# Left-over rows of a top-1 expert layer: grouped by expert over pairs of batches

## The chip, the cores and the metric

The kernel runs on one core of a Trainium2 chip. The metric is the time of one execution on the device in microseconds; what is compared is the median of several runs. The profile is one execution taken by the hardware profiler. Engines: PE multiplies matrices and writes PSUM banks, ACT, DVE and POOL work on vectors, SP issues most DMAs, POOL issues the indirect ones.

## The reference

Agent attention, then an expert layer in which each row goes to one expert:

```python
B, N, C = 4, 11456, 128        # 49 agents per batch; 8 experts, hidden size 1024
a2k = softmax(agents @ k.T / sqrt(C));  agent_v = a2k @ v       # 49 averages per batch
q2a = softmax(q @ agents.T / sqrt(C));  x = q2a @ agent_v       # one row per query
logits = x @ w_gate;  e = argmax(logits)
gate = softmax(logits)[e];  eom = 1 / (1 + exp(-(x @ w_output_gate)))
out = gate * eom[e] * (relu(x @ w1[e]) @ w2[e])                 # per row, by its expert e
```

## The kernel before

**Main stream.** For each batch the kernel picks one expert, the one that most rows choose, and computes all rows of the batch with it. A batch has 12 units of 1024 rows (the last has 192), a unit two tiles of 512. In a tile, `mm1` makes hidden values `h` from the softmax weights of the queries (`x_ld`) and the averages already multiplied into w1 (`w`); ACT writes `hh`, DVE the remainder `hl`; `mm2` multiplies both by w2 (`vv`) into `y`; ACT, DVE and POOL scale `y` into `os`, and SP stores it. Rows that belong to another expert ("left rows") get a wrong result here, and are written over later.

**Around it.** While a batch's main products run, the keys and values (`ks`, `av`) of the next batch and the queries (`qs`, then `q_rest`) of units ahead are worked on. A query unit may start once the main stream is at most four units behind it (`roomy`, `AHEAD = 5`). `q_rest` ends in a table of which rows chose which expert; `q_tail`, after a batch's last unit, counts them (`cum`, `tot`) and stores the running counts (`cumd`). The softmax weights of all rows go to DRAM (`efd`), and so do the 49 averages of a batch (`avnd`).

**Left rows.** They are gathered into tiles of 128 rows, one expert to a tile. `PHASES` holds (first batch, batches, static tiles, rows of the table): phase 0 is batches 0 to 2 with 13 tiles, phase 1 batch 3 with one. In a tile all rows are of one batch and one expert, so a phase has up to 8 groups for each of its batches. For a phase:

- `left_prepare` waits for the counts, calls `left_table` (which tile holds which group, and from which row of it on), and then `left_index` for 3, 4, 4 and 2 tiles at a time. These use the space of batch 3's key scores (`S0` to `S3`), so each call also waits until that part of the scores has been used. Phase 1 has one call.
- `left_index` finds for each of the 128 rows of a tile where it stands: the group's running counts by partition (product `pbs`), the partition and the rest by comparisons on DVE, a gather of a row of `cumd`, more comparisons, and a gather of the row's weights from `efd` into `ef`.
- `left_load` loads the averages of the tile's batch (`lav`) and the expert's w1 and w2 (`lw_ld`), for which it needs two of the 7 large load places that the loads of q, k and v use too. Those loads go first.
- `left_front` turns `ef` (product `let`) and multiplies it by the averages (`lx`, result `lxs`). `left_back` makes the hidden values (8 products `lh`) and the output (8 products `ly`), all in fp32. `left_store` scatters 128 rows to the output.

Two ways (`left_static`) each take every second tile, one after another. The last phase's `left_back` waits until the main stream has ended. Behind it stands a loop for tiles beyond the static ones.

**Order.** It is fixed when the program is built, by a planner. Each piece of work is a generator that asks for one instruction at a time; a clock of expected times (`Clock`) and priorities decide who goes next. Main products are emitted in turn, and `tick` puts at most one other fp32 product behind each. Relu work and the like has priority 0, `left_prepare` 1, `q_rest` 2, the fronts of left tiles 4, their backs 5. After an indirect DMA, score products (`block`) pause for 4.5 us.

Of the kernel before, what the change touches and what calls it, by code (L numbers as in the profile page):

```python
# [17 lines left out]
P = 128  # L18
# [11 lines left out]
PHASES = [(0, 3, 13, 384), (3, 1, 1, 128)]  # L30
# [15 lines left out]
K_OWN = 309  # L46
K_DUP = 310
K_W = 311
# [220 lines left out]
def agent_attention_top1_moe(ctx, tc, qT, kT, v, aT, wg, wo, w1, w2, cst, out):  # L269
# [94 lines left out]
    ticol = kc[:, K_TI:K_TI + 4]  # L364
# [1014 lines left out]
    def left_table(ph):  # L1379

        b0, nb, _, rows = PHASES[ph]
        ng, kr = nb * E, rows // P
        tt_ = tot[:, b0 * E:b0 * E + ng]

        def row(n, w=NG, dt=F32):
            return lt(n, [w], f"_{ph}", [min(w, ng)], dt)

        def cube(n):
            return lt(n, [4, NG], f"_{ph}", [kr, ng])
# [5 lines left out]
        ppi = row("ppi")  # L1395
# [6 lines left out]
        cnt = row("cntsb")  # L1402
# [10 lines left out]
        t0, ni, ti_ = row("t0"), row("t2"), row("t1i", NG, I32)  # L1413
# [3 lines left out]
        yield from DVE.q.tensor_tensor_scan(ni, ones[:, 0:ng], t0, 0.0, op0=ALU.mult, op1=ALU.add)  # L1417
        yield from DVE.q.tensor_scalar(ni, ni, 1.0 / 128.0, None, op0=ALU.mult)
        tt = lt(f"tt{ph}", [4, 8], f"_{ph}", [kr, 8])
        yield from POOL.q.memset(tt, 0.0)  # L1420
        ti = ticol[:, 0:kr]
        bc3 = [P, kr, ng]
# [5 lines left out]
        ne = lt("ne", [4], f"_{ph}", [kr])  # L1428
# [3 lines left out]
        yield from DVE.q.tensor_tensor(cm, iota32[:, 0:ng].unsqueeze(1).broadcast_to(bc3), g_.unsqueeze(2).broadcast_to(bc3), op=ALU.is_equal)  # L1432
        yield from DVE.q.tensor_tensor(cm2, cm, cnt.unsqueeze(1).broadcast_to(bc3), op=ALU.mult)
        yield from DVE.q.tensor_reduce(tt[:, :, 2], cm2, axis=AX.X, op=ALU.add)
        yield from DVE.q.tensor_scalar(g_, g_, float(ng - 1), None, op0=ALU.min)
# [7 lines left out]
        tti = lt("tti", [4, 8], f"_{ph}", [kr, 8], I32)  # L1443
# [3 lines left out]
        yield from DVE.q.tensor_copy(nti[ph], ni[:, ng - 1:ng])  # L1447

        yield from DVE.q.tensor_scalar(over[:, ph:ph + 1], ni[:, ng - 1:ng], float(PHASES[ph][2]), None, op0=ALU.is_gt)
# [3 lines left out]
    def left_index(ph, i, n, nm, got=None, big=None):  # L1453
# [11 lines left out]
        if own:  # L1465
# [12 lines left out]
            eq = lt("leq", [NSTM], nm, [n])  # L1478
# [6 lines left out]
            yield from PE.q.matmul(t[:, 0:n * P], ones[0:ng, :], c[0:ng].rearrange("p n k -> p (n k)"), start=True,  # L1485
                                   stop=True)
            yield from ACT.q.copy(pb.rearrange("p n k -> p (n k)"), t[:, 0:n * P])
            release(mark)
        else:
# [5 lines left out]
            gr = nc.values_load(ti[0:1, 0, 0:1], engines=[SP], min_val=0, max_val=ng - 1,  # L1495
                                skip_runtime_bounds_check_because=WHY)
            yield from SY.q.dma_start(pb[:, 0, :], ppid[ph][bass.ds(gr, 1), :].broadcast_to([P, P]))

        def col(m):
            return lt("l" + m, [NSTM], nm, [n])  # L1500
# [3 lines left out]
        yield from DVE.q.tensor_tensor(inv, r, tb[:, :, 2], op=ALU.is_ge)  # L1504
        rb = r.unsqueeze(2).broadcast_to([P, n, P])
# [4 lines left out]
        ppx = col("ppx")  # L1510
# [5 lines left out]
        yield from DVE.q.scalar_tensor_tensor(rg, tb[:, :, 0], 128.0, row, op0=ALU.mult, op1=ALU.add)  # L1516
        ru = lt("lru", [NSTM], nm, [n], U32)
# [20 lines left out]
        yield from DVE.q.scalar_tensor_tensor(t, tb[:, :, 4], float(N), t, op0=ALU.mult, op1=ALU.add)  # L1538
# [8 lines left out]
        o0 = n * NCOL  # L1547
# [5 lines left out]
        for k in range(n):  # L1553
# [3 lines left out]
            if got:  # L1557
                got(k, clk.ready[big.name] + (2000.0 if n > 1 else 0.0), ti, tg, ef, oa)
            yield from pause(1500.0 if n > 1 else 0.0)
        return ti, tg, ef, oa  # L1560

    def left_load(ph, ti, k, nm, at_=None):
        b0, nb, _, _ = PHASES[ph]
        yield from SY.wait(ti)
        er = nc.values_load(ti[0:1, k, 3:4], engines=[SP], min_val=0, max_val=E - 1,
                            skip_runtime_bounds_check_because=WHY)
        yield from SY.wait(ti)
        br = nc.values_load(ti[0:1, k, 4:5], engines=[SP], min_val=0, max_val=nb - 1,
                            skip_runtime_bounds_check_because=WHY)
        av = wk.tile([P, C], F32, name=f"lav{nm}", tag="l_av")  # L1570
        yield from SY.q.dma_start(av[0:A], avnd[b0:b0 + nb][bass.ds(br, 1)].rearrange("a p c -> p (a c)"))
# [10 lines left out]
        return av, w1t, w2t  # L1582
# [7 lines left out]
    def left_front(nm, ef, av):  # L1590
# [10 lines left out]
        yield from PE.q.matmul(x[:, 0:P], av[0:A], et[0:A], start=True, stop=True)  # L1601
# [37 lines left out]
    ready = {}  # L1639

    def left_prepare(ph):

        b0, nb, nst, _ = PHASES[ph]
        while counted[0] < b0 + nb:
            yield None
        yield from left_table(ph)
        i = 0
        for j, n in enumerate((3, 4, 4, 2) if nst > 2 else (nst,)):
# [7 lines left out]
            def got(k, t, ti, tu, ef, oa, i=i):  # L1656
                ready[ph, i + k] = t, ti, k, tu[:, k:k + 1], ef[:, k, :], oa[:, k, :]
# [11 lines left out]
    def left_static(way):  # L1669
# [8 lines left out]
        def fronts():  # L1678
            for i, (ph, k) in enumerate(todo):
                while (ph, k) not in ready or i > finished[0]:  # L1680
                    yield None
                t, ti, kk, _, ef, _ = ready[ph, k]
                yield from pause(t - clk.now())
                av, w1t, w2t = yield from left_load(ph, ti, kk, f"{ph}_{k}", left_place)
                yield from pause(max(clk.ready[x.name] for x in (av, w1t, w2t)) - clk.now())
                xs = yield from left_front(f"{ph}_{k}", ef, av)
# [3 lines left out]
        for ph, k in todo:  # L1690
# [5 lines left out]
            _, _, _, tu, ef, oa = ready[ph, k]  # L1696
# [48 lines left out]
    with tc.For_i(0, some, 1):  # L1745
        for ph, (b0, nb, nst, rows) in enumerate(PHASES):
            nr = nc.values_load(nti[ph][0:1, 0:1], min_val=0, max_val=rows,
                                skip_runtime_bounds_check_because="at most one tile per 128 tokens and one per group")
            with tc.For_i(nst, nr, 1) as i:
                ti, tu, ef, oa = drain(left_index(ph, i, 1, f"d{ph}"))  # L1750
                av, w1t, w2t = drain(left_load(ph, ti, 0, f"d{ph}"))
                xs = drain(left_front(f"d{ph}", ef[:, 0, :], av))
# [14 lines left out]
def _consts():  # L1767
# [42 lines left out]
```

## Time and profile before

| | |
|---|---|
| median of 3 runs | 976.49 us (975.86 to 976.65) |
| profiled execution, time | 976.57 us |
| profiled execution, span from first to last instruction | 974.8 us |
| mean granted clock of PE | 0.997 |
| busy: PE, DVE, ACT, POOL | 953.0, 788.0, 590.5, 352.5 us |
| largest group: y from hh, 2880 products | 526.6 us, 273 ns each |
| left tiles: lh and ly, 224 records each | 42.5 and 42.3 us busy |

An fp32 product appears as two records. Every instruction that goes through the planner carries line 219, so the profile is read by the names of tiles: `y<-vv,hl` is an instruction that writes y and reads vv and hl. In the groups, the number after the bar is the busy time in us, then the mean duration of one in ns, then the idle time of the engine just before, with what ended it.

### The profile page before, as it was taken

What the parts mean: (1) busy time and instruction counts of PE and PEld (TensorE: products, weight loads), DVE (VectorE), ACT (ScalarE), POOL (GpSimd) and SP (SyncE); (2) the same over time, 40 slices, a digit from 0 to 9 for tenths busy, and PEclk for the clock granted to TensorE, in tenths of its full rate; (3) what the DMA queues carried; (4) which work ended last, traced back from release to release, by engine and by line L of the source; (5) the groups of instructions that cost most, each with busy time, mean ns of one, the idle gap of its engine ahead of it and who ended that gap; (6) DMA issues with size and microseconds to landing.
All of it is one profiled execution on the core that took longest, in us unless ns stands there. A gap on an engine that the chain in (4) does not pass through costs nothing. (4 is left out here: it accounts for less than half of the span.)

```text
span 974.8 us, 37665 instructions
## 1 busy us (share of the span) xinstructions
PE 953.0 (98%) x15819; PEld 730.4 (75%) x15819; DVE 788.0 (81%) x2119; ACT 590.5 (61%) x1401; POOL 352.5 (36%) x629
## 2 busy tenths in 40 slices
PE   9999999999999999999999999999999999999996
PEld 7867777777777777776777777777777677888885
DVE  2878888989888887889878889889999878678652
ACT  2366666665766666667666666667566566555552
POOL 1013255552232364431323554521234354442221
PEclk9999999999999999999999999999999999999998
DMA  9986655646465655444566545444333453825420
GB/s 332 297 295 162 162 148 156 154 140 172 150 185 155 176 159 137 148 133 146 143 182 172 155 133 161 148 133 135 103 82 83 119 144 96 195 77 163 165 73 29
DMA packets 108899, 148.63 MB, mean 152 GB/s; under 512 B 62595, under 2 KB 71223, under 8 KB 108725
## 3 DMA queue, kind: packets, MB, share of 16 engines
q1 hardware_dynamic: 107380, 144.70, 51.5%
q8 instruction: 125, 2.05, 0.9%
q0 software_dynamic: 1344, 1.49, 0.8%
q14 instruction: 50, 0.40, 0.1%
HBM read 90.88 MB, written 35.17 MB: 129 GB/s over the span
## 5 line engine op out<-in xcount | busy, mean ns | idle before, releaser
L219 PE MATMUL y<-vv,hh 128*128 128x256 f16 (+1 forms) x2880 | 526.6, 273 | 5.2 <-DVE lL L219 2.3
L219 DVE SCALAR_TENSOR_TENSOR hl<-h,hh 128x512 f16<-128x512 f32 (+1 forms) x736 | 448.1, 667 | 93.1 <-ACT hh L219 90.7
L219 PE MATMUL y<-vv,hl 128*128 128x128 f16 (+1 forms) x2880 | 500.0, 219 | 1.5 <-DVE hl L219 0.9
L219 ACT ACTIVATE hh<-h 128x512 f16<-128x512 f32 (+1 forms) x736 | 372.1, 590 | 185.1 <-PE h L219 184.8
L219 PEld LDWEIGHTS <-hh 128*128 128x128 f16 (+1 forms) x2880 | 282.7, 98 | 56.9 <-issue 16.0
L219 PEld LDWEIGHTS <-hl 128*128 128x128 f16 (+1 forms) x2880 | 283.8, 99 | 9.5 <-issue 4.4
L219 PE MATMUL h<-x_ld,w 128*128 128x512 f16 (+1 forms) x1472 | 256.2, 376 | 0.7 <-DVE hl L219 0.4
L219 PEld LDWEIGHTS <-w 128*128 128x128 f16 x1472 | 83.5, 95 | 109.4 <-issue 72.9
L219 POOL TENSOR_TENSOR os<-os,smt 128x512 f32<-128x512 f32 (+1 forms) x91 | 94.9, 1042 | 114.1 <-DVE os L219 65.2
L219 ACT COPY ys<-y 128x256 f32<-128x256 f32 x179 | 67.6, 378 | 103.4 <-PE y L219 101.7
L219 DVE TENSOR_TENSOR os<-y,ys 128x256 f32<-128x256 f32 x179 | 74.2, 414 | 29.2 <-ACT ys L219 25.3
L219 POOL TENSOR_TENSOR e<-ef,e 128x392 f16<-128x392 f32 (+1 forms) x48 | 43.2, 899 | 67.8 <-ACT e L219 67.7
L219 POOL TENSOR_TENSOR ev<-S,km_o 128x400 f32<-128x400 f32 (+1 forms) x36 | 32.8, 914 | 58.2 <-PE av L219 53.9
L219 PEld LDWEIGHTS ks<-at,k_ld 128*32 128x32 f32 (+1 forms) x2316 | 39.9, 116 | 10.3 <-issue 7.8
L219 PE MATMUL ks<-at,k_ld 128*32 128x50 f32 (+1 forms) x2316 | 46.6, 213 | 0.7 <-DMA k_ld<-kT 0.6
L219 PE MATMUL qs<-at,q_ld 128*32 128x50 f32 (+1 forms) x2736 | 43.3, 210 | 0.0
L219 PEld LDWEIGHTS qs<-at,q_ld 128*32 128x32 f32 (+1 forms) x2736 | 36.5, 111 | 9.0 <-issue 8.0
L219 PE MATMUL lh<-lxs,lw_ld 128*128 128x128 f32 x224 | 42.5, 276 | 0.7 <-ACT lh L219 0.6
L219 PE MATMUL ly<-lw_ld,lh 128*128 128x128 f32 x224 | 42.3, 276 | 0.0
L219 POOL TENSOR_SCALAR smt<-lT,i 128x8 f32<-128x8 f32 (+1 forms) x48 | 15.5, 323 | 70.5 <-DVE lT L219 41.6
L219 POOL TENSOR_TENSOR og<-oh,ll 128x64 f32<-128x64 f32 (+1 forms) x48 | 16.3, 340 | 66.7 <-DVE oh L219 47.0
L219 ACT COPY S<-ks 128x400 f32<-128x400 f32 (+1 forms) x48 | 23.5, 490 | 23.2 <-PE ks L219 23.2
(252 smaller groups left out, 1012.8 us busy)
## 6 DMA issues: line engine op xcount, KB each, us to landing
v_ld<-v SPq DMA_DIRECT2D x44, 512.0 KB
q_ld<-qT SPq DMA_DIRECT2D x44, 512.0 KB
out<-os SPq DMA_DIRECT2D x88, 256.0 KB
k_ld<-kT SPq DMA_DIRECT2D x43, 512.0 KB
lw_ld<-w SPq DMA_DIRECT2D x28, 512.0 KB
efd<-ef SPq DMA_DIRECT2D x44, 200.0 KB
x_ld<-x_ld SPq DMA_DIRECT2D x132, 64.0 KB
w1t<-w SPq DMA_DIRECT2D x4, 512.0 KB
```

The lines of the kernel that those rows point to most:

```text
L219: return getattr(self.eng, op)(*a, **k)
```

## The change

The phases become two pairs of batches, (0, 1) with 12 static tiles and (2, 3) with one, and a tile holds rows of one expert from both batches of the pair, first those of the first batch. So a group's count is the sum over both (`cnt`), and the table keeps the first batch's share (`cnt0`, column 4). `left_index` takes three calls of 4 tiles in phase 0 instead of 3, 4, 4 and 2; it works out for each row which batch it is of (`bt`, and `two`, which has a one in the column of its batch), and builds the running counts with a small table of sides (`ls`) and one product for each tile. `left_front` writes the weights of a row into one of two halves (`xt`, 98 columns) on DVE, turns all 98 at once, and multiplies by the averages of both batches, which are loaded once per phase (`left_averages`) and not per tile. The loop for further tiles follows suit. The core of the diff:

```diff
-PHASES = [(0, 3, 13, 384), (3, 1, 1, 128)]
+PHASES = [(0, 2, 12, 256), (2, 2, 1, 256)]
...
     def left_table(ph):
...
-        yield from DVE.q.tensor_copy(cnt, cn_[:, 0:ng])
+        yield from DVE.q.tensor_copy(cnt0, cn_[:, 0:E])
+        yield from DVE.q.tensor_tensor(cnt, cn_[:, E:2 * E], cnt0, op=ALU.add)
...
-        if nb > 1:
-            yield from low_bits(tt[:, :, 3], g_, E - 1, lt("g_i", [4], f"_{ph}", [kr], I32))
-            yield from DVE.q.tensor_tensor(ne, g_, tt[:, :, 3], op=ALU.subtract)
-            yield from DVE.q.tensor_scalar(tt[:, :, 4], ne, 1.0 / E, None, op0=ALU.mult)
-        else:
-            yield from DVE.q.tensor_copy(tt[:, :, 3], g_)
+        yield from DVE.q.tensor_tensor(cm, cm, cnt0.unsqueeze(1).broadcast_to(bc3), op=ALU.mult)
+        yield from DVE.q.tensor_reduce(tt[:, :, 4], cm, axis=AX.X, op=ALU.add)
...
     def left_index(ph, i, n, nm, got=None, big=None):
...
-            yield from DVE.q.tensor_scalar(eq[0:ng], tb[0:ng, :, 0], pcol[0:ng], None, op0=ALU.is_equal)
-            yield from DVE.q.tensor_tensor(c[0:ng], ppt[0:ng].unsqueeze(1).broadcast_to([ng, n, P]),
-                                           eq[0:ng].unsqueeze(2).broadcast_to([ng, n, P]), op=ALU.mult)
+            yield from DVE.q.tensor_scalar(low[0:ng], tb[0:ng, :, 1], sign, None, op0=ALU.mult)
+            yield from DVE.q.scalar_tensor_tensor(low[0:ng], tb[0:ng, :, 4], sign, low[0:ng], op0=ALU.mult, op1=ALU.subtract)
+            yield from DVE.q.tensor_scalar(nd[0:ng], tb[0:ng, :, 0], expert, None, op0=ALU.not_equal)
+            yield from DVE.q.scalar_tensor_tensor(nd[0:ng], nd[0:ng], BIG, low[0:ng], op0=ALU.mult, op1=ALU.add)
+            yield from DVE.q.tensor_tensor(c[0:ng], side.unsqueeze(1).broadcast_to([ng, n, P]),
+                                           nd[0:ng].unsqueeze(2).broadcast_to([ng, n, P]), op=ALU.is_ge)
...
-            yield from PE.q.matmul(t[:, 0:n * P], ones[0:ng, :], c[0:ng].rearrange("p n k -> p (n k)"), start=True,
-                                   stop=True)
+            for k in range(n):
+                yield from PE.q.matmul(t[:, k * P:(k + 1) * P], c[0:ng, k, :], ppt[0:ng], start=True, stop=True)
...
+        yield from DVE.q.tensor_tensor(bt, r, tb[:, :, 4], op=ALU.is_ge)
+        yield from DVE.q.tensor_scalar(two[:, :, 0], bt, -1.0, 1.0, op0=ALU.mult, op1=ALU.add)
+        yield from DVE.q.tensor_tensor(ppx, bt, tb[:, :, 4], op=ALU.mult)
+        yield from DVE.q.tensor_tensor(r, r, ppx, op=ALU.subtract)
...
+        yield from DVE.q.scalar_tensor_tensor(rg, bt, 128.0 * E, rg, op0=ALU.mult, op1=ALU.add)
...
     def left_load(ph, ti, k, nm, at_=None):
...
-        av = wk.tile([P, C], F32, name=f"lav{nm}", tag="l_av")
-        yield from SY.q.dma_start(av[0:A], avnd[b0:b0 + nb][bass.ds(br, 1)].rearrange("a p c -> p (a c)"))
...
+    def left_averages(ph, nm):
+        b0, nb, _, _ = PHASES[ph]
+        av = wk.tile([P, C], F32, name=f"lav{nm}", tag="l_av")
+        yield from SY.q.dma_start(av[0:nb * A], avnd[b0:b0 + nb].rearrange("b a c -> (b a) c"))
+        return av
...
-    def left_front(nm, ef, av):
+    def left_front(nm, ef, xt, two, av):
+        yield from DVE.q.tensor_tensor(xt, ef[:, 0:A].unsqueeze(1).broadcast_to([P, 2, A]),
+                                       two.unsqueeze(2).broadcast_to([P, 2, A]), op=ALU.mult)
...
-        yield from PE.q.transpose(t[0:A, 0:P], ef[:, 0:A], idf)
+        yield from PE.q.transpose(t[0:2 * A, 0:P], xt.rearrange("p b k -> p (b k)"), idf)
...
-        yield from PE.q.matmul(x[:, 0:P], av[0:A], et[0:A], start=True, stop=True)
+        yield from PE.q.matmul(x[:, 0:P], av[0:2 * A], et[0:2 * A], start=True, stop=True)
...
     def left_prepare(ph):
...
+        if ph == 0:
+            yield from SY.q.dma_start(ls, sides)
+        averaged[ph] = yield from left_averages(ph, f"{ph}")
         yield from left_table(ph)
         i = 0
-        for j, n in enumerate((3, 4, 4, 2) if nst > 2 else (nst,)):
+        for j, n in enumerate((4, 4, 4) if nst > 2 else (nst,)):
```

More of the change, by code (lines that the diff above doesn't have):

```diff
@@ L45 @@
 K_TI = 305
-K_OWN = 309
-K_DUP = 310
-K_W = 311
+K_OWN = 307
+K_DUP = 308
+K_W = 309
 LANDS = 1500.0
@@ L268, in agent_attention_top1_moe @@
 @with_exitstack
-def agent_attention_top1_moe(ctx, tc, qT, kT, v, aT, wg, wo, w1, w2, cst, out):
+def agent_attention_top1_moe(ctx, tc, qT, kT, v, aT, wg, wo, w1, w2, cst, sides, out):
     nc = tc.nc
@@ L390, in agent_attention_top1_moe @@
         gss.append(t)
+    ls = cp.tile([2 * E, P + 2], F32, name="ls")
+    side, expert, sign = ls[:, 0:P], ls[:, P:P + 1], ls[:, P + 1:P + 2]
     oht = []
@@ L1383, in left_table, with row @@
         tt_ = tot[:, b0 * E:b0 * E + ng]
-        def row(n, w=NG, dt=F32):
-            return lt(n, [w], f"_{ph}", [min(w, ng)], dt)
+        def row(n, w=E, dt=F32):
+            return lt(n, [w], f"_{ph}", [w], dt)
         def cube(n):
-            return lt(n, [4, NG], f"_{ph}", [kr, ng])
+            return lt(n, [kr, E], f"_{ph}", [kr, E])
         yield from wait_free()
@@ L1394, in left_table @@
         yield from PE.q.matmul(pe_[:, 0:ng], tri, tt_, start=True, stop=True)
-        ppi = row("ppi")
+        ppi = row("ppi", ng)
         yield from DVE.q.tensor_tensor(ppi, pe_[:, 0:ng], tt_, op=ALU.add)
@@ L1401, in left_table @@
         yield from PE.q.matmul(cn_[:, 0:ng], ones, tt_, start=True, stop=True)
-        cnt = row("cntsb")
-        yield from DVE.q.tensor_copy(cnt, cn_[:, 0:ng])
+        cnt, cnt0 = row("cntsb"), row("cnt0")
+        yield from DVE.q.tensor_copy(cnt0, cn_[:, 0:E])
+        yield from DVE.q.tensor_tensor(cnt, cn_[:, E:2 * E], cnt0, op=ALU.add)
         release(mark)
@@ L1412, in left_table @@
         yield from SY.q.dma_start(ppid[ph], ppt[0:ng])
-        t0, ni, ti_ = row("t0"), row("t2"), row("t1i", NG, I32)
+        t0, ni, ti_ = row("t0"), row("t2"), row("t1i", E, I32)
         yield from DVE.q.tensor_scalar(ti_, cnt, 127.0, None, op0=ALU.add)
@@ L1416, in left_table @@
         yield from DVE.q.tensor_copy(t0, ti_)
-        yield from DVE.q.tensor_tensor_scan(ni, ones[:, 0:ng], t0, 0.0, op0=ALU.mult, op1=ALU.add)
+        yield from DVE.q.tensor_tensor_scan(ni, ones[:, 0:E], t0, 0.0, op0=ALU.mult, op1=ALU.add)
         yield from DVE.q.tensor_scalar(ni, ni, 1.0 / 128.0, None, op0=ALU.mult)
-        tt = lt(f"tt{ph}", [4, 8], f"_{ph}", [kr, 8])
+        tt = lt(f"tt{ph}", [kr, 8], f"_{ph}", [kr, 8])
         yield from POOL.q.memset(tt, 0.0)
         ti = ticol[:, 0:kr]
-        bc3 = [P, kr, ng]
+        bc3 = [P, kr, E]
         cm, cm2 = cube("cm"), cube("cm2")
@@ L1431, in left_table @@
         yield from DVE.q.tensor_scalar(tt[:, :, 1], ne, 128.0, None, op0=ALU.mult)
[L1432 removed]
+        yield from DVE.q.tensor_tensor(cm, iota8.unsqueeze(1).broadcast_to(bc3), g_.unsqueeze(2).broadcast_to(bc3), op=ALU.is_equal)
         yield from DVE.q.tensor_tensor(cm2, cm, cnt.unsqueeze(1).broadcast_to(bc3), op=ALU.mult)
         yield from DVE.q.tensor_reduce(tt[:, :, 2], cm2, axis=AX.X, op=ALU.add)
[L1435 to L1441 removed]
+        yield from DVE.q.tensor_tensor(cm, cm, cnt0.unsqueeze(1).broadcast_to(bc3), op=ALU.mult)
+        yield from DVE.q.tensor_reduce(tt[:, :, 4], cm, axis=AX.X, op=ALU.add)
+        yield from DVE.q.tensor_scalar(g_, g_, float(E - 1), None, op0=ALU.min)
         tables[ph] = tt, ppt
[L1443 removed]
+        tti = lt("tti", [kr, 8], f"_{ph}", [kr, 8], I32)
         yield from DVE.q.tensor_copy(tti, tt)
@@ L1446, in left_table @@
         yield from SY.q.dma_start(ttid[ph].rearrange("(k p) c -> p k c", p=P), tti)
-        yield from DVE.q.tensor_copy(nti[ph], ni[:, ng - 1:ng])
-        yield from DVE.q.tensor_scalar(over[:, ph:ph + 1], ni[:, ng - 1:ng], float(PHASES[ph][2]), None, op0=ALU.is_gt)
+        yield from DVE.q.tensor_copy(nti[ph], ni[:, E - 1:E])
+        yield from DVE.q.tensor_scalar(over[:, ph:ph + 1], ni[:, E - 1:E], float(PHASES[ph][2]), None, op0=ALU.is_gt)
     tables = {}
@@ L1494, in left_index @@
             yield from SY.wait(ti)
-            gr = nc.values_load(ti[0:1, 0, 0:1], engines=[SP], min_val=0, max_val=ng - 1,
+            gr = nc.values_load(ti[0:1, 0, 0:1], engines=[SP], min_val=0, max_val=E - 1,
                                 skip_runtime_bounds_check_because=WHY)
-            yield from SY.q.dma_start(pb[:, 0, :], ppid[ph][bass.ds(gr, 1), :].broadcast_to([P, P]))
+            yield from SY.q.dma_start(pb[:, 0, :], ppid[ph][0:E][bass.ds(gr, 1), :].broadcast_to([P, P]))
+            pb1 = big[:, 2 * P:3 * P]
+            yield from SY.q.dma_start(pb1, ppid[ph][E:2 * E][bass.ds(gr, 1), :].broadcast_to([P, P]))
         def col(m):
@@ L1504, in left_index @@
         yield from DVE.q.tensor_tensor(inv, r, tb[:, :, 2], op=ALU.is_ge)
+        two = lt("ltwo" + own, [rows_, 2], nm, [n, 2])
+        bt = two[:, :, 1]
+        yield from DVE.q.tensor_tensor(bt, r, tb[:, :, 4], op=ALU.is_ge)
+        yield from DVE.q.tensor_scalar(two[:, :, 0], bt, -1.0, 1.0, op0=ALU.mult, op1=ALU.add)
+        ppx = col("ppx")
+        yield from DVE.q.tensor_tensor(ppx, bt, tb[:, :, 4], op=ALU.mult)
+        yield from DVE.q.tensor_tensor(r, r, ppx, op=ALU.subtract)
+        if not own:
+            yield from DVE.q.tensor_tensor(pb1, pb1, pb[:, 0, :], op=ALU.subtract)
+            yield from DVE.q.scalar_tensor_tensor(pb[:, 0, :], pb1, bt, pb[:, 0, :], op0=ALU.mult, op1=ALU.add)
         rb = r.unsqueeze(2).broadcast_to([P, n, P])
@@ L1537, in left_index @@
         yield from DVE.q.tensor_tensor(t, t, f, op=ALU.add)
-        yield from DVE.q.scalar_tensor_tensor(t, tb[:, :, 4], float(N), t, op0=ALU.mult, op1=ALU.add)
+        yield from DVE.q.scalar_tensor_tensor(t, bt, float(N), t, op0=ALU.mult, op1=ALU.add)
         yield from DVE.q.scalar_tensor_tensor(t, inv, BIG, t, op0=ALU.mult, op1=ALU.add)
@@ L1546, in left_index @@
             yield from DVE.q.tensor_copy(tg, t)
-        o0 = n * NCOL
+        o0 = n * 2 * A
+        xt = big[:, 0:o0].rearrange("p (n b k) -> p n b k", b=2, k=A)
         o1 = o0 + n * A2
@@ L1557, in left_index @@
             if got:
-                got(k, clk.ready[big.name] + (2000.0 if n > 1 else 0.0), ti, tg, ef, oa)
+                got(k, clk.ready[big.name] + (2000.0 if n > 1 else 0.0), ti, tg, ef, oa, xt, two)
             yield from pause(1500.0 if n > 1 else 0.0)
-        return ti, tg, ef, oa
+        return ti, tg, ef, oa, xt, two
     def left_load(ph, ti, k, nm, at_=None):
@@ L1564, in left_load @@
         yield from SY.wait(ti)
-        er = nc.values_load(ti[0:1, k, 3:4], engines=[SP], min_val=0, max_val=E - 1,
+        er = nc.values_load(ti[0:1, k, 0:1], engines=[SP], min_val=0, max_val=E - 1,
                             skip_runtime_bounds_check_because=WHY)
-        yield from SY.wait(ti)
-        br = nc.values_load(ti[0:1, k, 4:5], engines=[SP], min_val=0, max_val=nb - 1,
-                            skip_runtime_bounds_check_because=WHY)
-        av = wk.tile([P, C], F32, name=f"lav{nm}", tag="l_av")
-        yield from SY.q.dma_start(av[0:A], avnd[b0:b0 + nb][bass.ds(br, 1)].rearrange("a p c -> p (a c)"))
         if at_ is None:
@@ L1593, in left_front @@
         mark = hold()
-        yield from PE.q.transpose(t[0:A, 0:P], ef[:, 0:A], idf)
+        yield from PE.q.transpose(t[0:2 * A, 0:P], xt.rearrange("p b k -> p (b k)"), idf)
         et = wk.tile([P, P], F32, name=f"let_sb{nm}", tag="l_et")
-        yield from ACT.q.copy(et[0:A], t[0:A, 0:P])
+        yield from ACT.q.copy(et[0:2 * A], t[0:2 * A, 0:P])
         release(mark)
@@ L1637, in agent_attention_top1_moe @@
     WAYS, LEFT = 2, 5
-    ready = {}
+    ready, averaged = {}, {}
     def left_prepare(ph):
@@ L1654, in left_prepare, with got @@
                 big = big.rearrange("p t a -> p (t a)")
-            def got(k, t, ti, tu, ef, oa, i=i):
-                ready[ph, i + k] = t, ti, k, tu[:, k:k + 1], ef[:, k, :], oa[:, k, :]
+            def got(k, t, ti, tu, ef, oa, xt, two, i=i):
+                ready[ph, i + k] = t, ti, k, tu[:, k:k + 1], ef[:, k, :], oa[:, k, :], xt[:, k], two[:, k, :]
             yield from left_index(ph, i, n, f"s{ph}_{i}", got, big)
@@ L1681, in fronts @@
                     yield None
-                t, ti, kk, _, ef, _ = ready[ph, k]
+                t, ti, kk, _, ef, _, xt, two = ready[ph, k]
                 yield from pause(t - clk.now())
-                av, w1t, w2t = yield from left_load(ph, ti, kk, f"{ph}_{k}", left_place)
-                yield from pause(max(clk.ready[x.name] for x in (av, w1t, w2t)) - clk.now())
-                xs = yield from left_front(f"{ph}_{k}", ef, av)
+                w1t, w2t = yield from left_load(ph, ti, kk, f"{ph}_{k}", left_place)
+                yield from pause(max(clk.ready[x.name] for x in (w1t, w2t)) - clk.now())
+                xs = yield from left_front(f"{ph}_{k}", ef, xt, two, averaged[ph])
                 ops[ph, k] = xs, w1t, w2t
@@ L1695, in left_static @@
                 yield None
-            _, _, _, tu, ef, oa = ready[ph, k]
+            _, _, _, tu, ef, oa, _, _ = ready[ph, k]
             yield from left_back(f"{ph}_{k}", *xs, oa, ef, ("lh", "ev")[way])
@@ L1749, in agent_attention_top1_moe @@
             with tc.For_i(nst, nr, 1) as i:
-                ti, tu, ef, oa = drain(left_index(ph, i, 1, f"d{ph}"))
-                av, w1t, w2t = drain(left_load(ph, ti, 0, f"d{ph}"))
-                xs = drain(left_front(f"d{ph}", ef[:, 0, :], av))
+                ti, tu, ef, oa, xt, two = drain(left_index(ph, i, 1, f"d{ph}"))
+                w1t, w2t = drain(left_load(ph, ti, 0, f"d{ph}"))
+                av = drain(left_averages(ph, f"d{ph}"))
+                xs = drain(left_front(f"d{ph}", ef[:, 0, :], xt[:, 0], two[:, 0, :], av))
                 drain(left_back(f"d{ph}", xs, w1t, w2t, oa[:, 0, :], ef[:, 0, :]))
@@ L1776, in _consts @@
     k[:, K_P] = i
-    k[:, K_TI:K_TI + 4] = i[:, None] + 128 * np.arange(4)
+    k[:, K_TI:K_TI + 2] = i[:, None] + 128 * np.arange(2)
     k[:, K_OWN] = i < 2 * A
@@ L1780, in _consts, with _sides @@
     return k
+def _sides():
+    import numpy as np
+    g = np.arange(2 * E)[:, None]
+    sign = np.where(g < E, -1.0, 1.0)
+    return np.concatenate([sign * (np.arange(P)[None] + 0.5), g % E, sign], axis=1).astype(np.float32)
 def kernel(q, k, v, agents, moe_w_gate, moe_w_output_gate, moe_w1, moe_w2):
@@ L1797 @@
         "cst": _consts(),
+        "sides": _sides(),
     }
```

9 lines of the change are left out of this document (4 added, 5 removed).

## The prediction, before the changed kernel was run

> **What bounds the kernel now.** I read the page first: span, busy shares, the forty slices.
>
> ```profile
> span 974.8 us, 37665 instructions
> PE 953.0 (98%) x15819; PEld 730.4 (75%) x15819; DVE 788.0 (81%) x2119; ACT 590.5 (61%) x1401; POOL 352.5 (36%) x629
> ...
> PE   9999999999999999999999999999999999999996
> ...
> DVE  2878888989888887889878889889999878678652
> ```
>
> PE is busy in every slice but the last, so a product taken out of it shortens the run nearly by its whole price, until something else ends last. Busy time overstates a product, because matmuls overlap. I therefore price a product by how far it pushes apart the starts of its neighbours, from the timeline of PE.
>
> The profiled execution took 976.57 us, 1.77 more than its span and 0.08 above the median of 976.49; the sum is made against it.
>
> The reference's routing gives the tiles. Rows whose expert is not the batch's commonest one number 705, 432, 0 and 37. They fill 8, 5, 0 and 1 tiles when grouped by batch and expert, and 6+4+1+1 = 12 and 1 when batches share an expert's tile. Both layouts fit their static tiles, so the loop for left-over tiles runs in neither. One tile of work goes.
>
> **The change part by part: PE.**
>
> ```profile
> 941.94 0.27 PE L219 MATMUL y<-vv,hh 128*128 128x256 f16 x1
> 942.05 0.39 PE L219 MATMUL ly<-lw_ld,lh 128*128 128x128 f32 x2
> ...
> 942.33 0.27 PE L219 MATMUL y<-vv,hh 128*128 128x256 f16 x1
> ...
> 945.46 0.27 PE L219 MATMUL y<-vv,hh 128*128 128x256 f16 x1
> ...
> 945.62 0.27 PE L219 MATMUL y<-vv,hh 128*128 128x256 f16 x1
> ...
> 954.59 0.27 PE L219 MATMUL y<-vv,hh 128*128 128x256 f16 x1
> 954.79 0.48 PE L219 MATMUL lx<-let_sb,lav 49*128 49x128 f32 x2
> ...
> 955.28 0.27 PE L219 MATMUL y<-vv,hh 128*128 128x256 f16 x1
> ```
>
> Two y steps start 0.16 us apart when nothing stands between them (945.46 to 945.62). With one fp32 product of a left tile between, it is 0.39. So one such product costs 0.225. With lx between, whose operands have 49 rows, it is 0.69: lx costs 0.525.
>
> ```profile
> 933.36 0.27 PE L219 MATMUL let<-kc,big 128*49 128x128 f32 x1
> 933.47 0.22 PE L219 MATMUL y<-vv,hl 128*128 128x128 f16 x1
> ...
> 771.40 0.27 PE L219 MATMUL y<-vv,hh 128*128 128x256 f16 x1
> 771.60 1.12 PE L219 MATMUL pbs<-big,ones 24*128 24x512 f32 x2
> ...
> 772.72 0.27 PE L219 MATMUL y<-vv,hh 128*128 128x256 f16 x1
> ...
> 920.16 0.27 PE L219 MATMUL y<-vv,hh 128*128 128x256 f16 x1
> 920.37 0.48 PE L219 MATMUL pbs<-bigs,ones 8*128 8x128 f32 x2
> ...
> 920.85 0.27 PE L219 MATMUL y<-vv,hh 128*128 128x256 f16 x1
> ```
>
> - One tile fewer. A tile is 8 lh and 8 ly products, one let and one lx: 16 x 0.225 + 0.11 + 0.525 = 4.2 us. **-4.2.**
> - lx over the averages of both batches: 98 rows where there were 49, in 13 tiles. No row has 98. The bounds are 0.525 (as with 49) and 0.225 (a full 128-row product of the same width). I take 0.225: the products with 49, 24 and 8 rows all start about 0.2 us after the y step before them where 0.11 is usual, and a 128-row product does not. 13 x 0.30 = **-3.9**, between -3.9 and 0.
> - pbs: one product per call of left_index becomes one per tile. Before, five calls: n = 4 costs 1.32 - 0.165 = 1.155 (771.40 to 772.72), n = 1 costs 0.525 (920.16 to 920.85), and n = 3 and 2, between these, 0.94 and 0.73: 4.5 in all. After, thirteen with 16 rows at 0.525, the price of the 8-row one: 6.8. **+2.3.**
> - let turns 98 columns instead of 49 into rows: 0.11 either way, since 128 columns stream in both; ±0. The call of left_index that goes takes its tbs product with it, 0.15; counted as nothing.
>
> Sum on PE: -5.8 us.
>
> The Trainium skill speaks on lx from two sides. "TensorEngine Tiling (Array Packing)", Key Properties, says that a change of tiling mode drains the engine; the extra 0.1 us ahead of lx agrees. "TensorE: Matmul & The Clock Gate", LDWEIGHTS, says that the rows of the stationary operand do not matter for its load, only the columns; by that lx would cost with 98 rows what it does with 49, and the sum would be -1.9 instead of -5.8. The rows above (0.525 against 0.225 at equal columns) speak against it; it is a rival below.
>
> **Off PE.** The 14 loads of averages (24.5 KB each) and their register loads leave SP's queue; two loads and that of the table of sides come in; SP is nowhere late. POOL loses one gather of each kind and one scatter; it is 36% busy. ACT's copy of let has 98 partitions instead of 49 at the same length. On DVE, each left tile gains one product of 98 elements a partition. Each call of left_index gains 8 small instructions on balance, and four calls stand where five stood; left_table comes out even. None is on the path while PE has work, with two exceptions.
>
> First, the index work moves. It needed batch 2's counts and now needs batch 1's and a free score tile, so it moves from after 675 us to about 560 to 760, beside the key and value work of batch 3.
>
> ```profile
> 575.00:600.00 25.00, 25.00 (x487) 19.28 (x486) 23.24 (x57) 16.66 (x39) 15.71 (x27) 1.00 0.48 141
> 600.00:625.00 25.00, 25.00 (x435) 18.42 (x433) 21.92 (x51) 15.76 (x37) 10.78 (x17) 1.00 0.43 122
> 625.00:650.00 25.00, 24.30 (x479) 18.46 (x477) 21.17 (x54) 15.51 (x37) 8.01 (x18) 1.00 0.48 140
> 650.00:675.00 25.00, 24.18 (x315) 17.50 (x313) 22.23 (x71) 16.44 (x42) 6.52 (x15) 1.00 0.57 168
> ...
> 700.00:725.00 25.00, 24.92 (x375) 18.60 (x373) 23.95 (x70) 15.80 (x41) 6.87 (x13) 1.00 0.43 117
> ```
>
> (Columns: stretch, its length, busy PE, weight load, DVE, ACT, POOL.) DVE has 1.8 to 3.8 us free in each 25 there. At 23.95 of 25, with index work in it, PE still lost nothing. The vector instructions of left_table and left_index add up to about 48 us between 675 and 925, an estimated 4.5 us in each 25 once the calls run one behind another; so the four stretches lack about 7 us between them. The bounds are 0 (the backlog is worked off after 675) and 7 (all reaches PE). I take 1.5, near the low end, because the 700 row shows PE whole beside a nearly full DVE. **+1.5.**
>
> Second, the end.
>
> ```profile
> 709.09 0.34 SPq L219 DMA_DIRECT2D q_ld<-qT  x1
> ...
> 725.88 0.52 PE L219 MATMUL qs<-at,q_ld 128*32 128x50 f32 x28
> ...
> 743.25 0.34 PE L219 MATMUL qs<-at,q_ld 128*32 128x50 f32 x12
> ...
> 774.32 0.27 PE L219 MATMUL let<-kc,big 128*49 128x128 f32 x1
> ...
> 859.14 0.27 PE L219 MATMUL let<-kc,big 128*49 128x128 f32 x1
> ...
> 851.40:961.50 110.10, 49.53 (x256) 40.83 (x257) 9.56 (x16) 1.00 0.35 113
> ...
> 851.36 1.35 PE L219 MATMUL h<-x_ld,w 128*128 128x512 f16 x8
> ...
> 858.32 0.38 PE L219 MATMUL qs<-at,q_ld 128*32 128x50 f32 x12
> ...
> 894.08 0.17 DVE L219 COPY tot<-cum 128x8 f32<-128x8 f32 x1
> ...
> 936.20 1.06 POOL L219 DMA_INDIRECT bigs<-efd,ltu_0s  x1 [5.31 <-issue]
> ...
> 952.28 0.27 PE L219 MATMUL let<-kc,bigs 128*49 128x128 f32 x1
> ...
> 955.31 0.27 ACT L219 COPY lxs<-lx 128x128 f32<-128x128 f32 x1 [1.33 <-PE lx L219]
> ...
> 961.52 2.00 PE L219 MATMUL lh<-lxs,lw_ld 128*128 128x128 f32 x16
> ```
>
> The last left tile, that of the last pair, may only start when the main products are through (961.52), and then 13.3 us remain to the span's end, which the change leaves alone. Its input (lxs) was ready 5.9 us earlier. It hangs on a chain that begins with the last query unit: scores (858.32, let go by the main work of unit 7 at 851.36), counts (894.08), table, index, gather (936.20), let, lx: 104 us from 851.36 to the end of lxs.
>
> The left tiles waited for their index until the first let (774.32). With the index done early, they can start when loads leave places for two weight tiles. The last q load (709.09) takes the place before; the query products at 725.88 and 743.25 free two more, so the first let comes near 750. From 859.14 to 933.36 one way takes three tiles, 24.7 us each. The row of the window, for the instructions on lh, has 256 records after 851.4, which at 32 a tile is 8 of 14 tiles. At that pace, and with the start 24 us earlier, I expect 3 to 4 of phase 0 there instead. The same stretch of main work then takes about 89 us instead of 110, and the chain must fit into 89 plus nothing.
>
> The chain shortens too. No index group of phase 0 runs beside it (estimate 4 to 8 us), and let no longer waits for an earlier tile of its way: 16 us lie between gather and let, of which I put 4 to 6 down to that. The last scores came 7 us after unit 7 and may come sooner (0 to 5). It lengthens by some ten dependent vector instructions (2 to 6). That makes 87 to 102 us: from in time to 13 us late. I take in time or up to 2 us late, **+0**, since the loss of competing work helps every link, and keep both ends.
>
> The sum: 976.57 - 5.8 + 1.5 = 972.3; with a little lateness, **973**.
>
> **The rivals.**
> - *The last tile comes late* (slower). If lxs is ready more than about 6 us after the main products end, the 5.8 us are gone. PE then idles, and its clock falls, as the granted clock shows after PE's last product here:
>
> ```profile
> 965.00:968.00 3.00, 0.51 (x5) 0.32 (x3) 0.00 (x0) 0.37 (x1) 1.01 (x1) 1.00 0.16 56
> 968.00:970.00 2.00, 0.00 (x0) 0.00 (x0) 0.00 (x0) 0.00 (x0) 0.00 (x0) 0.57 0.05 14
> ```
>
>  The 4 us of lh and ly could double. At 8 us late: 976.57 - 5.8 + 1.5 + 8 + 2 = 982. For it: the chain's middle estimate is only a little over 89. Against it: the 5.9 us of slack today, and the emptier engines.
> - *The same, partly*: 3 to 5 us late, 975 to 977.
> - *DVE bounds 560 to 700*: all 7 us reach PE: 976.57 - 5.8 + 7 = 977.8. For it: the DVE column above. Against it: the 700 row.
> - *lx is no cheaper with 98 rows*: the change does not do part of what it may: 976.57 - 1.9 + 1.5 = 976.2.
>
> **How the numbers follow.** Forecast (970.5 to 974.6): 0.45. Late by over 5: 0.27. Late in part: 0.13. DVE: 0.08. lx no cheaper: 0.07. About 0.2% (1.95 us) is what a measurement of this kernel can tell from no change, so the borders are 974.5 and 978.4. Faster 0.45; same 0.13 + 0.07 + some of DVE's, 0.23; slower 0.32. The range reaches from all of -5.8 and nothing back (970) to the late tile at 9 us (983).
>
> **What the next profile would show.** 208 lh records instead of 224, and lx with 98 rows pushing its neighbours 0.39 apart (right) or 0.69 (wrong). pbs as 26 records. let first near 750, and under 130 lh and ly records after unit 7 starts. DVE near 25 of 25 at 575 to 675, with PE's count of products down if it bounds. At the end, lh directly behind the last y if the tile is in time; a gap of PE there, and a clock under 1, if it is late. That gap is what would most likely make this wrong.

## The result, and the profile after

The kernel after takes **988.74 us** (median of 4 runs, 988.55 to 990.24), against 976.17 for the kernel before on the same chip (975.31 to 976.65): a ratio of 1.0136, with a 95% interval of 1.0121 to 1.0150. It is 12.6 us slower; 973 was forecast, and 983 was the upper end of the range. The profiled execution took 988.58 us with a span of 986.8.

The head of the page after, and two of its costliest groups:

```profile
span 986.8 us, 37491 instructions
PE 954.1 (97%) x15766; PEld 731.2 (74%) x15766; DVE 792.9 (80%) x2136; ACT 588.6 (60%) x1395; POOL 349.3 (35%) x625
...
L219 PE MATMUL y<-vv,hh 128*128 128x256 f16 (+1 forms) x2880 | 528.5, 274 | 7.8 <-ACT let_sb L219 2.0
...
L219 PE MATMUL lh<-lxs,lw_ld 128*128 128x128 f32 x208 | 40.6, 285 | 3.0 <-SPq L1766 2.9
```

PE is busy for 954.1 us, as before (953.0), but in a span 12 us longer. The last column (idle time just before a group, and what ended most of it) names two waits that the page before does not name: y products behind `let_sb`, 2.0 us (0.6 in the waits before), and lh behind SP's queue, 2.9 us (none before). The chain of work that ended last names only some 4 us (975.3 to 979.7), so I went on with the waits of PE over the whole run of the kernel after (us in total, times, longest):

```profile
PE lh L219 <- SPq L1766: 2.9, 1, 2.9
PE let L219 <- issue: 2.4, 1, 2.4
PE y L219 <- ACT let_sb L219: 2.0, 1, 2.0
PE let L219 <- DVE big L219: 1.7, 3, 0.7
```

All four belong to the left tiles. Two places hold them: the lets in the middle, and the last tile at the end.

**The middle.** PE and its neighbours around one let, in the timeline of the kernel after:

```profile
835.52 0.27 PE L219 MATMUL y<-vv,hh 128*128 128x256 f16 x1
836.31 0.25 DVE L219 TENSOR_TENSOR big<-big,ltwo_4s 128x98 f32<-128x98 f32 x1
...
836.66 0.29 PE L219 MATMUL let<-kc,big 128*98 128x128 f32 x1 [0.87 <-PE y L219]
...
836.79 0.22 PE L219 MATMUL y<-vv,hl 128*128 128x128 f16 x1
...
838.01 0.27 PE L219 MATMUL y<-vv,hh 128*128 128x256 f16 x1
838.12 0.39 PE L219 MATMUL lx<-let_sb,lav 98*128 98x128 f32 x2
838.34 0.22 PE L219 MATMUL y<-vv,hl 128*128 128x128 f16 x1
838.40 0.27 PE L219 MATMUL y<-vv,hh 128*128 128x256 f16 x1
```

At 835.52 PE has nothing left to do but let, and let needs xt, the new DVE product, which only starts at 836.31. The row names PE's own y as releaser, but y had long ended; the DVE row above it is what let waited for. Worked out as in the prediction (how far a let pushes its neighbours apart), the 12 lets of the main work cost 6.4 us, 0.12 to 1.15 each, where 12 before cost 1.3. Seven of them wait: they start 0.06 to 0.15 us after the end of their xt, and cost 0.43 or more. lx below it is as forecast: two y steps 0.39 apart (838.01 to 838.40).

**The end.** The last tile in the kernel after; before, lh stood directly behind the last y at 961.52:

```profile
965.35 1.05 POOL L219 DMA_INDIRECT bigs<-efd,ltu_0s  x1 [7.71 <-issue]
...
965.67 0.22 PE L219 MATMUL y<-vv,hl 128*96 128x128 f16 x1
...
967.88 0.26 DVE L219 TENSOR_TENSOR bigs<-bigs,ltwo_0s 128x98 f32<-128x98 f32 x1 [0.37 <-DMA bigs<-efd,ltu_0s]
...
968.25 0.29 PE L219 MATMUL let<-kc,bigs 128*98 128x128 f32 x1 [2.36 <-issue]
...
968.64 0.95 SPq L219 DMA_DIRECT2D lw_ld<-w  x2
...
969.72 0.27 ACT L219 COPY lxs<-lx 128x128 f32<-128x128 f32 x1 [0.88 <-PE lx L219]
...
972.63 3.41 PE L219 MATMUL lh<-lxs,lw_ld 128*128 128x128 f32 x16 [2.94 <-SPq L1766]
...
978.62 1.04 POOL L219 DMA_INDIRECT out<-bigs,ltg_0s  x1 [11.13 <-ACT bigs L219]
```

The last gather is issued (965.35) as the last y is about to start (965.67). Everything behind it runs on an empty PE: xt, let, lx, then 2.9 us until the two weight tiles, which are only asked for at 968.64, are there. lh starts 7 us after the last y, and its 16 records take 3.41 us where 2.00 is usual. From the last y to the end of the span it is 21.1 us, 7.8 more than before (961.46 to 974.80).

### The profile page after: what moved, and what is told of

Its sections match the earlier page's. It is cut to its first block, busy times and chain, and to the rows that moved or that the text cites. A ratio compares the mean times of both kernels' runs of the same rounds, so it can differ in the third digit from the quotient of the medians.

```text
span 986.8 us, 37491 instructions
## 1 busy us (share of the span) xinstructions
PE 954.1 (97%) x15766; PEld 731.2 (74%) x15766; DVE 792.9 (80%) x2136; ACT 588.6 (60%) x1395; POOL 349.3 (35%) x625
## 5 line engine op out<-in xcount | busy, mean ns | idle before, releaser
L219 PE MATMUL ly<-lw_ld,lh 128*128 128x128 f32 x208 | 39.2, 276 | 0.0
L219 PEld LDWEIGHTS lh<-lxs,lw_ld 128*128 128x128 f32 x208 | 33.4, 200 | 4.3 <-issue 3.2
```

Of the source, the lines that this page charges most:

```text
L219: return getattr(self.eng, op)(*a, **k)
```

## The experiments

The kernel before took 975.9 to 976.3 us in every set of runs, so medians are compared directly. Three theories. **A**: let waits for xt. The planner's clock leaves the index buffer (`big`) out, since gathers and readers share it (`clk.apart`); xt lies in that buffer, so the planner knows no due time for it and puts let right behind it. **B**: the end; too little work stands beside the last tile's chain, and its weights are asked for too late. **C**: the index work beside batch 3's keys and values.

### Where it is lost: both kernels without the last tile

```diff
-        todo = [(ph, k) for ph, x in enumerate(PHASES) for k in range(x[2])][way::WAYS]
+        todo = [(0, k) for k in range(PHASES[0][2])][way::WAYS]
...
-        for _ in range(sum(x[2] for x in PHASES)):
+        for _ in range(PHASES[0][2]):
```

> The kernel after without the front, products and scatter of the last left tile (its table, index and gathers stay); its 37 rows are left out. What remains ends with the stores of the last main unit. To be held against the same cut of the kernel before. Theory B (all of the 12.5 us are lost behind the last tile): 969 to 970, as the kernel before with the same cut. Theories A and C (the middle loses too: last y at 965.7 against 961.5): about 973 to 974, 4 us above the cut kernel before. By the prediction's sum it would be 5 us below that.

> The kernel before with the same cut: no front, products and scatter of its last left tile. The last y ends at 961.5 in the whole kernel, and the stores behind it take some 8 us: about 969 to 970. If the last tile's chain had slowed the main work before it, 1 to 3 us less than that.

977.06 us (974.51 to 979.12) and 971.82 (970.85 to 972.39). So with the same cut, which leaves the 37 rows of the last tile out, the kernel after is 5.2 us slower, and the two ranges do not overlap. The last tile itself adds 988.74 - 977.06 = 11.7 us after and 976.17 - 971.82 = 4.4 before: 7.3 more. Both places are real. (That 5.2 + 7.3 is the whole loss follows from the way the two numbers are formed.) By the forecast's sum the cut kernel after should have been the faster one by 4 to 5.

### Theory A: xt in a tile of its own

```diff
     def left_front(nm, ef, xt, two, av):
+        xt = wk.tile([P, 2, A], F32, name=f"lxt{nm}", tag="l_xt")
         yield from DVE.q.tensor_tensor(xt, ef[:, 0:A].unsqueeze(1).broadcast_to([P, 2, A]),
```

> Only change against the kernel after: the product xt that let turns gets a tile of its own instead of a part of the index buffer, so that the program that orders the instructions knows when xt is due and puts let later on PE. Theory A (let waits for xt: the twelve lets in the main work push their neighbours 0.4 to 1.1 us apart, median 0.78, where it was 0.11 before): let falls back to about 0.11 to 0.2, some 6 us of PE come back in the middle, the last y ends at about 960 instead of 965.7, and the time falls from 988.7 to about 983 to 984. Theory B (the end is set by the last tile's chain of DVE and gathers, whatever PE does in the middle): the last y ends earlier, but the gap before the last let grows from 2.5 to about 7 us, and the time stays at 987 to 989. Theory C (the index work beside batch 3's keys and values is what costs): no change of either.

**976.22 us** (974.08 to 977.77), a ratio of 0.9999 to before (0.9990 to 1.0009). One line takes back all 12.5 us, more than any of the theories said. (The profiled execution took 974.73, 1.5 below the median.) The lets (count, least/median/most duration, first and last start) and all that waited for them:

```profile
L219 PE MATMUL let<-kc,lxt x13: 271/273/322, 769.1 to 956.0; 128*98 128x128 f32 x13
its engine sat idle before it (us, times) until:
who waited for it (us, times):
  ACT let_sb L219: 1.9, 6
```

No wait of PE ahead of any let is left; in the kernel after the same view lists five kinds. From the end of xt to its let there are now 0.54 to 3.5 us, so it is the place of let that the due time changed. By their neighbours all 13 cost 2.1 us. And the last tile is in time: its gather went out at 946.2, xt ran at 954.6, lxs at 957.9, and lh directly behind the last y:

```profile
955.90 0.13 PEld L219 LDWEIGHTS let<-kc,lxt 128*98 128x98 f32 x1
956.01 0.27 PE L219 MATMUL let<-kc,lxt 128*98 128x128 f32 x1
...
957.86 0.27 ACT L219 COPY lxs<-lx 128x128 f32<-128x128 f32 x1 [0.29 <-PE lx L219]
...
959.87 2.00 PE L219 MATMUL lh<-lxs,lw_ld 128*128 128x128 f32 x16
```

Why should the end profit from it? With lets put later the left tiles run later, so main unit 7 of batch 3, which lets go the last query unit, starts at 864.1 instead of 876.0. That explanation needed a test without the cure of let.

### Theory B: left tiles held back, and the last weights early

Held back alone (fronts of way 0 and 1, the last three tiles of each):

```diff
             for i, (ph, k) in enumerate(todo):
+                while ph == 0 and i >= 3 and mains[0] < 84:
+                    yield None
```

> Only change against the kernel after: the last six of the twelve left tiles are held back until the main work of unit 7 of batch 3 has begun. xt stays where it is, lets still wait. So six to seven tiles instead of under four stand behind that unit, which starts 7 to 10 us earlier, and the last query unit with it. Theory B (the last tile is late because too little work stands beside its chain): lh follows the last y at once, the 7 us of the tail go, and the time falls from 988.7 to 980 to 982. If the chain is late for another reason (its own length, DVE): it moves with the stretch, and the time stays at 987 to 989.

985.18 us (984.89 to 986.63): 3.6 us less, about half of what was expected. Unit 7 does start at 864.4, and the stretch behind it grows. The window from unit 7 to the last y, for PE's instructions on lh, in this kernel and in the kernel after (length, PE busy and records):

```profile
864.40:965.30 100.90, 37.19 (x192) 1.00 0.31 106
```

```profile
876.00:965.70 89.70, 20.25 (x105) 1.00 0.21 69
```

The gather comes at 956.3, in time. But xt does not follow it. DVE in that kernel:

```profile
966.03 0.35 DVE L219 SCALAR_TENSOR_TENSOR os<-y,smt,ys 96x128 f32<-96x128 f32 x1 [2.27 <-ACT ys L219]
966.81 0.35 DVE L219 SCALAR_TENSOR_TENSOR os<-y,smt,ys 96x128 f32<-96x128 f32 x1 [0.43 <-ACT ys L219]
967.08 0.25 DVE L219 TENSOR_TENSOR bigs<-bigs,ltwo_0s 128x98 f32<-128x98 f32 x1
```

DVE has time, but in its fixed order xt stands behind the last stores. The front waits, in the planner's time, for the weights of its tile before it asks for xt; so weights asked for late put xt late, too. That was tried alone and together. Alone, the weights of the last tile loaded as soon as the table's row is read:

```diff
+            if ph == 1:
+                spawn(last_load(), 1)      # left_load(1, ti, 0, ...) once ti is written
...
-                w1t, w2t = yield from left_load(ph, ti, kk, f"{ph}_{k}", left_place)
+                if ph == 1:
+                    w1t, w2t = early[0]
+                else:
+                    w1t, w2t = yield from left_load(ph, ti, kk, f"{ph}_{k}", left_place)
```

> Only change against the kernel after: the two weight tiles of the last left tile are loaded as soon as its expert is known (about 30 us before the end) and not after its last gather. Theory B1 (at the end lh waits 2.9 us behind lx for these loads, after a chain that is late already): lh follows lx by about 1.0 us instead of 2.9, and the time falls from 988.7 to about 986.5. If it was the lowered clock or the copy lxs that held lh: no change, 988.7.

985.62 us (985.30 to 988.20, the highest being the profiled one), 1.0100 of before (1.0083 to 1.0116): 3.1 us gone. lh now follows lxs at once, and the wait that ends before it is ACT's copy:

```profile
971.04 0.27 ACT L219 COPY lxs<-lx 128x128 f32<-128x128 f32 x1 [0.88 <-PE lx L219]
...
971.36 3.79 PE L219 MATMUL lh<-lxs,lw_ld 128*128 128x128 f32 x16 [0.35 <-ACT lxs L219]
```

Both edits together:

> The kernel after with both edits of e7_hold_left and e2_early_load: six left tiles held back until unit 7, and the last tile's weights loaded as soon as its expert is known. In e7_hold_left the last gather was issued at 956.3, 9 us ahead of the last y, but the product xt, and with it let, stood behind the last stores' work until 967.1, since the front waits for its weights. Theory B: with the weights early xt and let move ahead of the last y, lh follows it at once, and 2.5 to 3.5 us go: 985.2 to about 982. That would be the kernel before plus the 5 us of the middle. If xt stays late: 985.

**979.08 us** (978.52 to 982.41), 1.0036 of before (1.0025 to 1.0047). The end is closed, with lets still waiting:

```profile
963.84 0.29 PE L219 MATMUL let<-kc,bigs 128*98 128x128 f32 x1 [0.44 <-PE y L219]
...
966.82 0.22 PE L219 MATMUL y<-vv,hl 128*96 128x128 f16 x1
966.88 2.00 PE L219 MATMUL lh<-lxs,lw_ld 128*128 128x128 f32 x16
```

So the end is worth 988.74 - 979.08 = 9.7 us, a little more than the 7.3 of the cut kernels. What is left to e1_xt_own, which has neither of these edits and lets that do not wait, is 2.9 us by the two medians and 3.6 by the two ratios. By their neighbours the lets of the two profiles differ by 7.9 - 2.1 = 5.8; that profiled execution took 981.54, 2.5 above its median. Theories A and B are both shown, and they share a part, since alone they give 12.5 and 9.7 of 12.6 us: late lets also moved the end.

### Theory C: the index back at its old place

```diff
-        while counted[0] < b0 + nb:
+        while counted[0] < max(b0 + nb, 3):
```

on top of e1_xt_own.

> The kernel after with xt in a tile of its own (as in e1_xt_own) and with the table and index of batches 0 to 2 held back until batch 2 is counted, as in the kernel before. e1_xt_own still lost 3.3 us on PE against its sum (av, lg, h and y rows, a wait of 1.06 us at 682.5) and ran at 973.0 by its profile, 976.2 by its median. Theory C (index work beside batch 3's keys and values is what these 3 us are): the first main unit of batch 3 starts near 707 instead of 711.5, and the time falls by 2 to 4 us, to 972 to 974. Rival D (the index, held back, gates the left tiles group by group again and runs beside the last tile's chain): what is won ahead of 712 is lost behind it, 976 to 981.

975.44 us (972.95 to 977.25), 0.9991 of before (0.9981 to 1.0001), which overlaps with e1_xt_own. Unit 0 of batch 3 starts at 706.6, as theory C says, against 711.5. But it is given back, as rival D says, though at another place than D named: not at the last chain, but between 675 and 775, where DVE is near full. The waits of PE there in this kernel, and the one that the kernel before has on hl there:

```profile
PE y L219 <- DVE hl L219: 3.0, 3, 1.3
```

```profile
PE y L219 <- DVE hl L219: 0.5, 1, 0.5
```

Most of the 4.9 us ahead of 711.5 was no loss at all: 24 pbs records, 5.0 us on PE, had only moved there from behind 706, and 128 qs records (1.6 us) the other way. Within these intervals the place of the index work is not what costs.

### What e1_xt_own still loses

Its first let meets a full queue of ACT. PE in that kernel, with the granted clock of the 50 us around it:

```profile
769.39 0.22 PE L219 MATMUL y<-vv,hl 128*128 128x128 f16 x1
771.62 0.37 PE L219 MATMUL y<-vv,hh 128*128 128x256 f16 x1 [2.01 <-ACT let_sb L219]
```

```profile
750.00:800.00 50.00, 46.66 (x618) 34.38 (x616) 41.19 (x106) 29.35 (x73) 21.82 (x43) 0.97 0.49 123
```

The y at 771.62 needs the bank that let's copy sets free, and the copy stands on ACT behind four hh copies and three more. Behind that gap the granted clock was 0.5 from 771.6 to 775.0. So the first left tile was held back; its let moved from 769.1 to 788.0, twice as far as was meant:

```diff
             for i, (ph, k) in enumerate(todo):
+                while mains[0] < 77:
+                    yield None
```

> The kernel of e1_xt_own (xt in a tile of its own), with the first left tile of each way held back until the second half of unit 3 of batch 3 has begun, about 9 us. There the first let holds a bank whose release, the copy on ACT, stands behind three copies that wait for products behind the let on PE: PE lost 2.0 us at 771 and ran slower until 774, and the granted clock of 750 to 800 is 0.97. If that meeting is chance and costs what it shows: the gap and the dip go, 2 to 3.5 us come back, and the time falls from 976.2 to 972.5 to 974. If the next let meets the same queue: no change, 976.

974.60 us (973.30 to 976.21), 0.9983 of before (0.9974 to 0.9992): 1.6 us less than e1_xt_own, with intervals that still overlap. The dip of the clock is gone and the wait behind let's copy shrank from 2.0 to 0.9 us, but there is a gap of 1.8 us that ends at 795.7, behind work of DVE, so both expectations hold in part:

```profile
750.00:800.00 50.00, 46.06 (x629) 32.94 (x626) 43.42 (x106) 30.67 (x74) 21.39 (x39) 1.00 0.43 118
```

### lx alone, in the kernel before

```diff
-        av = wk.tile([P, C], F32, name=f"lav{nm}", tag="l_av")
+        av = avz[turn[0] % 2]          # two tiles, zeroed once; likewise etz for let_sb
...
-        yield from PE.q.matmul(x[:, 0:P], av[0:A], et[0:A], start=True, stop=True)
+        yield from PE.q.matmul(x[:, 0:P], av[0:2 * A], et[0:2 * A], start=True, stop=True)
```

> The kernel before with one part of the change alone: lx multiplies 98 rows instead of 49, the added ones zero (the two operands lie in tiles that are zeroed once). No tile less, no index moved. By the prediction's rows (0.225 against 0.525 us a product, 14 of them) the time falls by 3.9 to 4.2 us, from 976.2 to about 972; lx pushes its neighbours 0.39 us apart. If rows do not matter: 976.2.

**971.88 us** (971.34 to 973.17), 0.9960 of before (0.9946 to 0.9973): 4.4 us less, where 3.9 to 4.2 were expected. It is the fastest kernel here that computes all rows, faster than before and after. PE and its weight loads (PEld) in it, around one lx (two y steps 0.39 apart):

```profile
801.31 0.27 PE L219 MATMUL y<-vv,hh 128*128 128x256 f16 x1
801.31 0.30 PEld L219 LDWEIGHTS lx<-etz,avz 98*128 98x128 f32 x2
801.42 0.39 PE L219 MATMUL lx<-etz,avz 98*128 98x128 f32 x2
...
801.64 0.22 PE L219 MATMUL y<-vv,hl 128*128 128x128 f16 x1
...
801.70 0.27 PE L219 MATMUL y<-vv,hh 128*128 128x256 f16 x1
```

And the weight load of lx in the kernel before, where the y step ahead of it starts at 954.59:

```profile
954.79 0.29 PEld L219 LDWEIGHTS lx<-let_sb,lav 49*128 49x128 f32 x2 [0.16 <-issue]
```

With 98 rows the load starts together with the y step ahead, 0.11 us before the product; with 49 it starts only with the product, 0.20 after that y step. That is 0.1 of the 0.29 us; the rest lies behind the start of the product, from which the next y follows after 0.42 us instead of 0.22. One load record takes about as long in both, 184 ns with 49 rows and 191 with 98.

## Why the prediction was wrong

The direction was wrong, and two steps made it so. Point by point:

- **PE's own products (-5.8): right.** lx with 98 rows costs 0.223, where 49 rows cost 0.511; e8_before_lx98 shows the same by time. By the Trainium skill ("TensorE: Matmul & The Clock Gate", LDWEIGHTS), the time of a weight load goes by its columns and not by its rows; the trace agrees for the load itself (184 ns against 191). What did not hold is the inference that the whole product then costs the same, which gave -1.9. A pbs product of 16 rows costs 0.509 (0.525 was taken), five calls 4.6 (4.5), thirteen products 6.6 (6.8). The records are 208 lh, 26 pbs, as listed.
- **"let ... 0.11 either way; ±0": the first failed step.** The product as such does cost 0.11 (the lets that do not wait). But the prediction had put xt on DVE among the instructions that are "none on the path". It asked what DVE's time is worth, not who waits for the product: PE is in order, let stands in PE's queue, and the planner did not know when xt would be done. That wait costs 6.4 - 1.3 = 5.1 us in the profile, and 2.9 to 3.6 by time between e9_hold_and_load and e1_xt_own.
- **Not foreseen: the first let at a full ACT.** 2.0 us (771.0 to 773.0). The granted clock of the kernel after was at half twice in the middle:

```profile
709.30:712.72 3.42, 3.42 (x23) 2.75 (x23) 2.27 (x12) 0.59 (x1) 0.40 (x1) 0.50 0.29 53
774.16:777.57 3.41, 3.41 (x22) 1.92 (x21) 1.59 (x4) 2.07 (x5) 0.23 (x1) 0.50 0.43 82
```

  The second stretch stands behind this gap, as in e1_xt_own; e10_xt_hold_first has a gap of 1.8 us and none, so what sets it off stays open. The first stands ahead of all products of left tiles. Up to the first let, PE's products come in the same order in the kernel after and in e1_xt_own, which has 1.00 there and reaches that let 1.4 us earlier (769.1 against 770.5): these 1.4 us are clock, not order.
- **Index work beside batch 3 (+1.5): about right.** Up to unit 0 of batch 3 the PE products of e1_xt_own take 1.5 to 1.9 us more than before once the moved pbs and qs are set aside. DVE was not at its limit there (20.3 to 23.6 of 25 us in the four stretches, in the kernel after); it put off other work (last `av` at 681 instead of 652).
- **The end (+0, with 0 to 13 late as bounds): the second failed step.** The stretch behind unit 7 was forecast as 89 us, and it is 89.7; the chain as 87 to 102, and it is 94 (876.0 to the end of lxs at 970.0). So the tile is 4.3 us late in the bounds given, and taking "in time" out of 87 to 102 against 89 was a choice against its own middle. But the reason for the short stretch was another than stated: the first let is at 770.5, not near 750; the tiles then follow every 12.4 us instead of every 13.3, and more of them run ahead of unit 7, which starts at 876.0 instead of 851.4. And one term was missing: the weight loads, which had been hidden behind 5.9 us of slack, became a wait of 2.9 us of their own, where the prediction had SP "nowhere late". With PE idle its clock fell, as the rival said (0.5 from 970 to 975).

The rival "the last tile comes late" (982) was the nearest; it had the end right and lacked the lets. From the forecast's 972.3, the lets (5.1), the first let (2.0), the end (7.8) and the index (0.4 above its 1.5) give 987.6; the profiled execution took 988.58. The half clock at 709 and at 774 is not in that sum, and the first alone is 1.4 us, so the terms agree with the run within 1 or 2 us and no better.

## What to carry to other kernels

When an in-order engine is full, ask of each new instruction elsewhere not only whether its engine has time but which instruction of the full engine waits for it, and whether whoever fixes the order knows when it is due; a buffer that the planner was told to ignore hides every due time in it. When work moves ahead, look at what it covered: here left tiles that ran earlier uncovered the last tile's chain, and loads that were asked for after that chain became a second wait. A part of a change can be worth more alone: padding one product to 98 rows gave 4.4 us without any regrouping.

## What the runs showed of the hardware that was not expected

- After some microseconds with nothing but let and lx PE came back slow. Such a stretch lasts from the last y to lh, 7.0 us in the kernel after and 4.5 in e2_early_load, and the 16 lh records behind it took 3.41 and 3.79 us; directly behind the last y they took 2.00 (e1_xt_own, e9_hold_and_load). The granted clock was 0.50 from 971 to 975 in e2_early_load, and in the kernel after 0.71 from 972.6 to 977.6:

```profile
972.60:977.60 5.00, 4.97 (x31) 5.00 (x32) 0.00 (x0) 1.19 (x2) 0.00 (x0) 0.71 0.24 92
```

- One DVE product of 128x128, on the last tile's chain, took 1.09 us in the kernel after, where it takes 0.29 in e1_xt_own. It stands beside a POOL product that had started 0.1 us earlier, and ends about when that one does:

```profile
949.47 1.04 POOL L219 TENSOR_TENSOR os<-os,smt 128x512 f32<-128x512 f32 x1 [8.15 <-issue]
949.56 1.09 DVE L219 TENSOR_TENSOR bigs<-bigs 128x128 f32<-128x128 f32 x1
```

  So it is in all five kernels that keep xt in the index buffer (1.09 to 1.10 us). In the other six no POOL product stands there, and it takes 0.29. No run moved the POOL product alone.
